# Weight words of block 0 in a PSUM bank, three column tiles converted ahead

## The chip, the cores and the metric

The kernel runs on one core of one Trainium2 chip. The metric is the device time of one execution in microseconds, lower is better. The program is compiled once and run several times; the median counts. A profile is taken in an execution of its own.

## The reference

Three layers follow each other, for 2 sequences of 768 tokens and 512 channels (1536 tokens in all):

```
attention:  8 heads of 64; each token sees the last 128 tokens and the first 4 of its sequence
            scores = q k^T / 8, softmax over the kept ones, times v
dense FFN:  h = x @ w_in        (512 -> 2048)
            g = max(0.01 h, h)
            x = g @ w_out       (2048 -> 512)
router:     8 experts, each token goes to the best one (at most 384 tokens an expert)
            y = gate * relu(x @ w1[e]) @ w2[e]    (512 -> 1024 -> 512)
```

The weights of the dense layer, `w_in` and `w_out`, arrive as 64-bit floats. [...]

## The kernel before

The tokens are cut into 6 blocks of 256 (two tiles of 128). The attention of later tiles and the dense layer of earlier blocks run interleaved: the loop over blocks j holds a loop over 16 column tiles f of the hidden layer, and between them the steps of the attention pipeline are called, so that block 0 of the dense layer works while attention is at tiles 2 and 3. The order on TensorE, ScalarE, GpSimd and SyncE is that of the code; VectorE's order is made by the scheduler of the framework from priorities and dependencies, and then it is a plain queue as well.

In block 0 the dense layer multiplies in full 32-bit form with the converted weights. For column tile f, `first` (L817) forms the product `hps` in a PSUM bank, `leak` (L832) lets ScalarE write 0.01 h (L837) and VectorE the maximum `g` (L838), and two tiles later `second` (L852) adds g times `w_out` to the two banks `y`. From block 1 on the weights are split into two halves `wh` and `wl` (L797, L798).

`convert` (L758) makes the words of column tile f: x = 0 is the piece of `w_in` (raw tile `rawi`), x = 1 that of `w_out` (`rawo`), each 128 x 512 words. Three VectorE operations build a word in place in an SBUF tile `cvt`: `low_word` (L769) shifts and masks the high half, `sign` (L773) ors the sign bit in, `tail` (L777) ors in the top bits of the low half. The six operations of a tile are issued step by step, x = 0 and x = 1 in turn, so that no operation needs the result of the one just before it. They are given a lower priority by `BEHIND` places. `START` names the attention steps at which a conversion begins ahead of block 0; in block 0 one more tile is begun in each of the 16 iterations, so the conversion runs two tiles ahead of the product. The raw tiles have 4 buffers, two column tiles; SyncE loads a pair (0.5 MB each) as soon as the conversion of the pair two tiles before has let go of them.

PSUM has 8 banks: 4 in the pool `ps` for attention, 2 for `y` (`psy`), 2 for `hps` (`psh`). The scores of the first two attention tiles ("plain" ones, `scores_plain`, L635) use `psh` or `psy` before block 0 needs them.

Of the kernel before, what the change touches and what calls it, by code (L numbers as in the profile page):

```python
# [8 lines left out]
F32 = mybir.dt.float32  # L9
F32R = mybir.dt.float32r  # L10
BF16 = mybir.dt.bfloat16
I32 = mybir.dt.int32
AF = mybir.ActivationFunctionType
ALU = mybir.AluOpType
AX = mybir.AxisListType
PSUM = bass.MemoryType.PSUM
DRAM = bass.MemoryType.DRAM

P = 128
# [10 lines left out]
HQ = 3  # L30
SINK = (2, 6)
ROUTER = 3
START = (4, 5)
WARM = 10


RAW = 4
BEHIND = (100, 20)
LAG = 2
SPLIT = (1, 2)  # L40
CLEAR_AT, CLEAR = 8, 2
# [346 lines left out]
class RingAttention(Attention):  # L388
# [246 lines left out]
    def scores_plain(self, t, g):  # L635

        nc = self.nc
        n = t + 1
        mx = self.p["sm"].tile([P, 2, 2], F32, tag="mx", name="mx")
        pss = []  # L640
        for e in range(2):
            d = slice(64 * e, 64 * e + 64)
            if (t * self.NG + g) % 2:
                ps = self.p["psy"].tile([P, 2, n, P], F32, tag=f"y{e}", name="sps")
            else:
                ps = self.p["psh"].tile([P, 2, n, P], F32, tag="h", name="sps")
            for pr in range(2):
                for x in range(n):
                    nc.tensor.matmul(ps[:, pr, x, :], lhsT=self.ident_b, rhs=self.mp[t][:, x * P:(x + 1) * P],
                                     start=True, stop=False)  # L650
                    nc.tensor.matmul(ps[:, pr, x, :], lhsT=self.qk[t, g][d, 2 + pr, :], rhs=self.qk[x, g][d, pr, :],  # L651
                                     start=False, stop=True)
            nc.vector.reduce_max(mx[:, e, :], ps.rearrange("p a n c -> p a (n c)"), axis=AX.X, negate=True)
            nc.vector.tensor_scalar(out=mx[:, e, :], in0=mx[:, e, :], scalar1=self.scale, scalar2=None, op0=ALU.mult)
            pss.append(ps)
        self.pu[t, g] = (pss, mx)
# [58 lines left out]
class FFN:  # L715
# [39 lines left out]
            out=ri, in_=A["moe_w_in"].rearrange("(k p) c -> p k c", p=P)[:, :, f * P * u:(f + 1) * P * u])  # L755
        self.raw[f, x] = ri.rearrange("p k c -> p (k c)")

    def convert(self, f):  # L758

        nc, c = self.nc, self.p["c"]  # L760
        if f >= self.NF:
            return []
        v, w = {}, {}

        def low_word(x):
            r = self.raw[f, x]
            w[x] = r.rearrange("p (n two) -> p n two", two=2)
            v[x] = c.tile([P, 512], I32, tag="c", name="cvt")
            nc.vector.tensor_scalar(v[x], w[x][:, :, 1], 3, 0x3FFFFFF8, op0=ALU.logical_shift_left,  # L769
                                    op1=ALU.bitwise_and)  # L770

        def sign(x):
            nc.vector.scalar_tensor_tensor(v[x], w[x][:, :, 1], -0x40000000, v[x], op0=ALU.bitwise_and,  # L773
                                           op1=ALU.bitwise_or)

        def tail(x):
            nc.vector.scalar_tensor_tensor(v[x], w[x][:, :, 0], 29, v[x], op0=ALU.logical_shift_right,  # L777
                                           op1=ALU.bitwise_or)

        def take(x):  # L780
            r = self.raw.pop((f, x))
            if not self.wide:
                v[x] = c.tile([P, 512], F32, tag="c", name="cvt")
                nc.vector.tensor_copy(v[x], r)
            self.v[f][x] = v[x].bitcast(F32)

        self.v[f] = {}
        calls = [low_word, sign, tail, take] if self.wide else [take]
        return [lambda g=g, x=x: g(x) for g in calls for x in range(2)]

    def split(self, f, x, eng):

# [39 lines left out]
    def leak(self, j, f):  # L832

        nc, N = self.nc, self.N
        ps = self.g[j, f]
        g = self.p["g"].tile([P, N], F32, tag="g", name="g")
        nc.scalar.activation(g, ps, AF.Copy, scale=0.01)  # L837
        nc.vector.tensor_tensor(out=g, in0=ps, in1=g, op=ALU.max)  # L838
        self.g[j, f] = g
# [577 lines left out]
def build(tc, A, n_sink, window, capacity):  # L1417
    nc = tc.nc
# [10 lines left out]
    def pool(st, name, **kw):  # L1429
        p[name] = st.enter_context(tc.tile_pool(name=name, **kw))  # L1430

    with ExitStack() as es:

        work, att, rawst, psy, psh, pst = (ExitStack() for _ in range(6))
        pool(es, "dram", bufs=1, space=DRAM)
        pool(es, "const", bufs=1)
        pool(es, "sm", bufs=3)
# [1 line left out]
        pool(work, "g", bufs=LAG + 1, side="right")  # L1439
        pool(pst, "ps", bufs=4, side="right", space=PSUM)  # L1440
        pool(psy, "psy", bufs=1, side="right", space=PSUM)
        pool(psh, "psh", bufs=2, side="right", space=PSUM)
        es.enter_context(tc.manual_schedule(engines=ORDERED))
        ident = p["const"].tile([P, P], F32, name="ident")
        make_ident(nc, ident)
# [19 lines left out]
        def step(*between):  # L1465

            nonlocal done
            d, pre, mid = steps.pop(0) if steps else (None, (), ())
            for f in (*pre, *between, *mid):
                f()  # L1470
            if d is not None:
                done = d
# [19 lines left out]
        nraw = RAW if ring else 2  # L1492
        pool(rawst, "raw", bufs=nraw, side="right")

        ffn = FFN(nc, p, A, xt, FFN.CAP if ring else FFN.CAP - FEWER // 4)
# [4 lines left out]
        def convert():  # L1500

            nonlocal chunk
            n, chunk = chunk, chunk + 1
            def later(f):
                with tc.high_priority(offset=-BEHIND[started]):
                    f()

            return [lambda f=f: later(f) for f in ffn.convert(n)] + [lambda: [ffn.load(2 * n + nraw + x) for x in range(2)]]

        def some(calls, n):  # L1510
            for f in calls[:n]:
                f()
            del calls[:n]

        conv, started = [], 0
        rt = None
        for n in range(len(steps)):
            if done == TPB - 1:
                break
            if n == ROUTER:  # L1520
                rt = Router(nc, p, A, capacity, ident)
            if n in START:
                conv += convert()
            step(lambda: some(conv, 3))
            some(conv, 3)
        some(conv, 99)
        while chunk < 2:
            some(convert(), 99)
        rt = rt or Router(nc, p, A, capacity, ident)
        started = 1  # L1530
# [16 lines left out]
        def split(n, f=-1, x=0):  # L1547

            while splits and (n > 0 or f >= 0 and x not in ffn.w.get(f, ())):
                ffn.split(*splits.pop(0), nc.vector if j else nc.gpsimd)  # L1550
                n -= 1
# [30 lines left out]
        for j in range(NB):  # L1582
            need = TPB * (j + 2) - 1
            count = next((n + 1 for n, x in enumerate(steps) if x[0] == need), len(steps))
            ndone = 0
            early = j == late and rt.NU
            if j == late:
                att.close()
            if early:
                pool(es, "mx", bufs=1)  # L1590
                ex.start_x()
            for i, f in enumerate(ffn.order(j)):
                if j == 0:
                    conv += convert()
                if j == 1:
                    split(0, f, 0)
                ffn.first(j, f)
                leak = lambda: (some(conv, 2), ffn.leak(j, f), some(conv, 2))
                if ndone < min(count, count * (i + 1) // (ffn.NF - 1)):
                    step(leak)  # L1600
                    ndone += 1
                else:
                    leak()
                more = lambda: ndone < min(count, count * (i + 1) // (ffn.NF - 1))
                some(conv, 2)
                ffn.split_g(j, f, j == late and i >= ffn.NF - ENDG)
                pending.append((j, f, i))
                if len(pending) > LAG:
                    second()
                while more():  # L1610
                    step()
                    ndone += 1
                some(conv, 99)
                split(SPLIT[min(j, 1)])
                if j > 0 or i >= CLEAR_AT:
                    some(clears, max(1, rate) if j else CLEAR)
                if routing and i in ROUTE:
                    routing.pop(0)()
                if early:
                    ex.room = min(ex.RAW + ex.PARTS, 6 + 4 * max(0, i - 1) - (0 if ring else FEWER))  # L1620
                    ex.refill(2)
                    if i == 6:
                        ex.get(0, 0)
                    if i == 11:
                        px = p["ps"].tile([P, DM // P, P], F32, tag="att", name="px")
                        ex.turn(0, 0, px)
                        ex.x_parts(0, 0, px)
            if j == 0:
                rawst.close()
                pool(es, "rt", bufs=2)  # L1630
        def tail():
# [74 lines left out]
```

## Time and profile before

| | |
|---|---|
| median of 3 runs | 650.66 us (650.65 to 652.32) |
| profiled execution | 657.48 us, span 655.8 us |
| TensorE busy in the span | 615.8 us, 94% |
| VectorE busy in the span | 433.5 us, 66% |
| ScalarE, GpSimd busy | 344.9 us, 251.9 us |
| VectorE busy from 60.9 to 143.8 us | 75.09 of 82.9 us |
| TensorE busy from 143.8 to 200 us | 55.59 of 56.2 us |

Busy shares over the whole span mix stages with different limits; a stage is read from a window of its own. Busy times of TensorE have modelled ends, so that 94% is not 94% of its peak. PE is TensorE, DVE is VectorE, ACT is ScalarE, POOL is GpSimd, SP is SyncE. L769 is line 769 of the kernel.

### The profile page before, as it was taken

What the parts mean: (1) busy time and instruction counts of PE and PEld (TensorE: products, weight loads), DVE (VectorE), ACT (ScalarE), POOL (GpSimd) and SP (SyncE); (2) the same over time, 40 slices, a digit from 0 to 9 for tenths busy, and PEclk for the clock granted to TensorE, in tenths of its full rate; (3) what the DMA queues carried; (4) which work ended last, traced back from release to release, by engine and by line L of the source; (5) the groups of instructions that cost most, each with busy time, mean ns of one, the idle gap of its engine ahead of it and who ended that gap; (6) DMA issues with size and microseconds to landing.
All of it is one profiled execution on the core that took longest, in us unless ns stands there. A gap on an engine that the chain in (4) does not pass through costs nothing.

```text
span 655.8 us, 12403 instructions
## 1 busy us (share of the span) xinstructions
PE 615.8 (94%) x4057; PEld 531.2 (81%) x4057; DVE 433.5 (66%) x1031; ACT 344.9 (53%) x997; POOL 251.9 (38%) x451
## 2 busy tenths in 40 slices
PE   9998687989999999999999999999999999996995
PEld 7685555658899999999999998997788888985774
DVE  1499999968986567666766662277366666545871
ACT  4474456558765666655666553255244444434641
POOL 5357596655544545444544443132101001010030
PEclk9598799889999999999999999999899999999898
DMA  9147866942164521141114005756256665446800
GB/s 254 22 147 230 268 190 210 280 134 70 50 241 147 155 56 49 34 145 34 36 39 144 3 10 176 258 177 212 67 182 206 217 201 181 146 132 196 276 14 13
DMA packets 83710, 91.82 MB, mean 140 GB/s; under 512 B 43171, under 2 KB 51363, under 8 KB 83616
## 3 DMA queue, kind: packets, MB, share of 16 engines
q1 hardware_dynamic: 81536, 85.58, 43.1%
q0 software_dynamic: 2080, 5.13, 2.2%
q8 instruction: 41, 0.67, 0.5%
q14 instruction: 53, 0.43, 0.2%
HBM read 71.91 MB, written 20.48 MB: 141 GB/s over the span
## 4 chain that ended last, share of the span: by engine, by line
PE 60%; DVE 17%; issue 9%; ACT 5%; DMA 5%; POOL 2%; SPq 0%; another core or an unknown queue 0%; DVEq 0%; POOLq 0%; ACTq 0%
PE y L867 13%; PE hps L829 13%; PE py L1284 9%; PE ph L1237 8%; PE ops L300 4%; DVE cvt L777 3%; DVE cvt L773 3%; DMA out<-ys,gt 2%; PE sps L651 2%; PE sps L520 2%; DMA craw<-in_moe_w 2%; DVE cvt L769 2%; DVE g L838 2%; PE lps L950 1%; DVE wl L798 1%
## 5 line engine op out<-in xcount | busy, mean ns | idle before, releaser
L867 PE MATMUL y<-wh,gp 128*128 128x512 f32 x320 | 115.1, 400 | 1.0 <-ACT gp L847 1.0
L849 POOL TENSOR_TENSOR gp<-g,gp 128x256 fp32r<-128x256 f32 x77 | 56.8, 738 | 141.9 <-ACT gp L847 129.5
L829 PE MATMUL hps<-xth,wh 128*128 128x256 f32 x320 | 92.7, 290 | 0.0
L1284 PE MATMUL py<-cw,ht 128*128 128x512 f32 x336 | 84.7, 406 | 6.5 <-DVE ht L1274 6.5
L829 PE MATMUL hps<-xtl,wh 128*128 128x256 f32 x320 | 90.2, 282 | 0.0
L829 PE MATMUL hps<-xth,wl 128*128 128x256 f32 x320 | 90.0, 281 | 0.0
L1129 DVE TENSOR_TENSOR cw<-craw,cw 128x512 fp32r<-128x512 f32 x128 | 82.8, 691 | 9.1 <-ACT cw L1127 7.8
L1284 PEld LDWEIGHTS py<-cw,ht 128*128 128x128 f32 x336 | 63.3, 193 | 21.9 <-DVE ht L1274 8.2
L1293 POOL DMA_INDIRECT out<-ys,gt x14 | 17.4, 1244 | 163.8 <-DVE ys L1292 149.5
L1127 ACT CAST cw<-craw 128x512 fp32r<-128x512 f32 x112 | 63.5, 620 | 30.7 <-PE py L1284 30.1
L838 DVE TENSOR_TENSOR g<-hps,g 128x256 f32<-128x256 f32 x96 | 40.2, 418 | 51.5 <-ACT g L837 43.0
L867 PEld LDWEIGHTS y<-wh,gp 128*128 128x128 f32 x320 | 60.0, 188 | 12.3 <-ACT gp L847 1.9
L837 ACT ACTIVATE g<-hps 128x256 f32<-128x256 f32 x96 | 36.4, 379 | 55.1 <-PE hps L829 55.0
L829 PEld LDWEIGHTS hps<-xtl,wh 128*128 128x128 f32 x320 | 60.3, 188 | 3.1 <-issue 0.7
L829 PEld LDWEIGHTS hps<-xth,wh 128*128 128x128 f32 x320 | 60.3, 189 | 3.0 <-issue 0.7
L867 PE MATMUL y<-wl,gp 128*128 128x512 f32 x160 | 62.6, 391 | 0.0
L829 PEld LDWEIGHTS hps<-xth,wl 128*128 128x128 f32 x320 | 60.6, 189 | 0.0
L1237 PE MATMUL ph<-xt,cw 128*128 128x256 f32 (+2 forms) x444 | 58.2, 291 | 1.2 <-DVE xt L1227 0.8
L1237 PEld LDWEIGHTS ph<-xt,cw 128*128 128x128 f32 x444 | 56.6, 189 | 2.0 <-DVE xt L1227 1.5
L213 ACT ACTIVATE pm<-pm,mx 128x132 f32<-128x132 f32 (+1 forms) x80 | 31.7, 398 | 44.3 <-DVE mx L533 44.0
L847 ACT CAST gp<-g 128x256 fp32r<-128x256 f32 x80 | 32.7, 409 | 38.4 <-DVE g L838 31.1
L300 PE MATMUL ops<-pt,vt 128*64 128x128 f32 x456 | 40.8, 233 | 4.9 <-POOL pt L568 4.7
(197 smaller groups left out, 1329.4 us busy)
## 6 DMA issues: line engine op xcount, KB each, us to landing
craw<-in_moe_w SPq DMA_DIRECT2D x128, 256.0 KB
rawi<-in_moe_w_in SPq DMA_DIRECT2D x16, 512.0 KB
rawo<-in_moe_w_out SPq DMA_DIRECT2D x16, 512.0 KB
places<-zero SPq DMA_DIRECT2D x24, 257.0 KB
wh<-wscr SPq DMA_DIRECT2D x16, 256.0 KB
wl<-wscr SPq DMA_DIRECT2D x16, 256.0 KB
xg<-places SPq DMA_DIRECT2D x14, 257.0 KB
natv<-in_v SPq DMA_DIRECT2D x12, 256.0 KB
```

What stands on the lines that cost most here:

```text
L213: nc.scalar.activation(pm[:, e, 0:w], pm[:, e, 0:w], AF.Exp, bias=mx[:, e:e + 1], accum_out=su[:, e:e + 1])
L300: nc.tensor.matmul(ps[:, e, :], lhsT=l, rhs=r, start=(x == 0), stop=(x == len(mm) - 1))
L829: nc.tensor.matmul(ps, lhsT=w, rhs=x, start=(n == 0), stop=(n == len(mm) - 1))
L837: nc.scalar.activation(g, ps, AF.Copy, scale=0.01)
L838: nc.vector.tensor_tensor(out=g, in0=ps, in1=g, op=ALU.max)
L847: nc.scalar.copy(gp[:, 0], g)
L849: eng.tensor_tensor(out=gp[:, 1], in0=g, in1=gp[:, 0].bitcast(F32), op=ALU.subtract)
L867: nc.tensor.matmul(y, lhsT=l, rhs=r, start=(start and n == 0), stop=(stop and n == len(mm) - 1))
L1127: nc.scalar.copy(h, t)
L1129: eng.tensor_tensor(out=l, in0=t, in1=h.bitcast(F32), op=ALU.subtract)
L1237: nc.tensor.matmul(self.ph[f][:, sl], lhsT=w, rhs=self.xt[:, a, k, sl], start=(m == 0), stop=(m == 3 * self.K - 1), skip_group_check=True)
L1284: nc.tensor.matmul(self.py[n], lhsT=x, rhs=w, start=(h == 0 and f == 0 and m == 0), stop=(h == self.NH - 1 and f == self.HF - 1 and m == 2))
```

## The change

In block 0 the word is built in a PSUM bank: `low_word` writes the bank, `sign` works in place there, and `tail` reads it and writes the SBUF tile `cvt`. There is one such bank, and the two words of a column tile are now made one after the other, not in turn. Ahead of block 0 the words are made in SBUF as before, but three column tiles are begun there (START) and not two, so that the conversion runs three tiles ahead. The priority offset in block 0 is 100 instead of 20. The bank is taken from `psh`: in block 0 the product `hps` has one bank, and from block 1 on two again. The plain scores that used the two banks of `psh` in turn take one bank each for their two halves.

```diff
-START = (4, 5)
+START = (3, 4, 5)
...
-BEHIND = (100, 20)
+BEHIND = (100, 100)
...
-                ps = self.p["psh"].tile([P, 2, n, P], F32, tag="h", name="sps")
+                ps = self.p[("psh", "psc")[e]].tile([P, 2, n, P], F32, tag="hu"[e], name="sps")
...
-    def convert(self, f):
+    def convert(self, f, bank):
...
-        v, w = {}, {}
+        v, w, u = {}, {}, {}
 
         def low_word(x):
             r = self.raw[f, x]
             w[x] = r.rearrange("p (n two) -> p n two", two=2)
-            v[x] = c.tile([P, 512], I32, tag="c", name="cvt")
-            nc.vector.tensor_scalar(v[x], w[x][:, :, 1], 3, 0x3FFFFFF8, op0=ALU.logical_shift_left,
+            if bank:
+                u[x] = self.p["psc"].tile([P, 512], I32, tag="u", name="word")
+            else:
+                u[x] = v[x] = c.tile([P, 512], I32, tag="c", name="cvt")
+            nc.vector.tensor_scalar(u[x], w[x][:, :, 1], 3, 0x3FFFFFF8, op0=ALU.logical_shift_left,
                                     op1=ALU.bitwise_and)
 
         def sign(x):
-            nc.vector.scalar_tensor_tensor(v[x], w[x][:, :, 1], -0x40000000, v[x], op0=ALU.bitwise_and,
+            nc.vector.scalar_tensor_tensor(u[x], w[x][:, :, 1], -0x40000000, u[x], op0=ALU.bitwise_and,
                                            op1=ALU.bitwise_or)
 
         def tail(x):
-            nc.vector.scalar_tensor_tensor(v[x], w[x][:, :, 0], 29, v[x], op0=ALU.logical_shift_right,
+            if bank:
+                v[x] = c.tile([P, 512], I32, tag="c", name="cvt")
+            nc.vector.scalar_tensor_tensor(v[x], w[x][:, :, 0], 29, u[x], op0=ALU.logical_shift_right,
                                            op1=ALU.bitwise_or)
...
-        return [lambda g=g, x=x: g(x) for g in calls for x in range(2)]
+        return [lambda g=g, x=x: g(x) for x in range(2) for g in calls]
...
-        pool(psh, "psh", bufs=2, side="right", space=PSUM)
+        pool(psc, "psh", bufs=1, side="right", space=PSUM)
+        pool(psc, "psc", bufs=1, side="right", space=PSUM)
...
-            return [lambda f=f: later(f) for f in ffn.convert(n)] + [lambda: [ffn.load(2 * n + nraw + x) for x in range(2)]]
+            return [lambda f=f: later(f) for f in ffn.convert(n, started)] + [lambda: [ffn.load(2 * n + nraw + x) for x in range(2)]]
...
             if j == 0:
+                psc.close()
+                pool(psh, "psh", bufs=2, side="right", space=PSUM)
                 rawst.close()
```

The lines behind it move: in the changed kernel `low_word`, `sign` and `tail` are L773, L777 and L783, and the maximum is L844. The orders of TensorE, ScalarE and GpSimd stay as they were, and on SyncE one pair of raw loads moves ahead. On VectorE the conversions move. The first place is the start of block 0, from the casts `kT`, which free a bank for attention, to the first maximum `g`. Before:

```order
L163 CAST kT_122<-kps 128x4x4 x2
L777 SCALAR_TENSOR_TENSOR cvt<-rawo,cvt 128x512
L769 TENSOR_SCALAR cvt<-rawi 128x512
L769 TENSOR_SCALAR cvt<-rawo 128x512
L773 SCALAR_TENSOR_TENSOR cvt<-rawi,cvt 128x512
L773 SCALAR_TENSOR_TENSOR cvt<-rawo,cvt 128x512
L838 TENSOR_TENSOR g<-hps,g 128x256
```

The same place on VectorE now, where `word` is the bank:

```order
L163 CAST kT_125<-kps 128x4x4 x2
L777 SCALAR_TENSOR_TENSOR cvt<-rawi,cvt 128x512
L773 TENSOR_SCALAR cvt<-rawo 128x512
L783 SCALAR_TENSOR_TENSOR cvt<-rawi,cvt 128x512
L777 SCALAR_TENSOR_TENSOR cvt<-rawo,cvt 128x512
L777 SCALAR_TENSOR_TENSOR word<-rawi,word 128x512
L783 SCALAR_TENSOR_TENSOR cvt<-rawo,cvt 128x512
L783 SCALAR_TENSOR_TENSOR cvt<-rawi,word 128x512
L773 TENSOR_SCALAR word<-rawo 128x512
L844 TENSOR_TENSOR g<-hps,g 128x256
```

Eight conversion operations stand between the casts and the first maximum instead of five, and by then tile 2 is complete and four of the six operations of tile 3 are done. The second place is the middle of block 0 on VectorE, with buffer numbers. Before, the piece from the sixth maximum:

```order
L838 TENSOR_TENSOR g_901<-hps_881,g_901 128x256
L769 TENSOR_SCALAR cvt_897<-rawi_805 128x512
L769 TENSOR_SCALAR cvt_899<-rawo_807 128x512
L773 SCALAR_TENSOR_TENSOR cvt_897<-rawi_805,cvt_897 128x512
L773 SCALAR_TENSOR_TENSOR cvt_899<-rawo_807,cvt_899 128x512
L532 COPY_PREDICATED pm_921<-sel_174,sps_923 128x128
L532 COPY_PREDICATED pm_921<-sel_174,sps_924 128x128
L777 SCALAR_TENSOR_TENSOR cvt_897<-rawi_805,cvt_897 128x512
L533 TENSOR_REDUCE mx_922<-pm_921 128x2
L777 SCALAR_TENSOR_TENSOR cvt_899<-rawo_807,cvt_899 128x512
```

A piece of the changed kernel's middle, around the seventh maximum:

```order
L777 SCALAR_TENSOR_TENSOR word_1033<-rawi_896,word_1033 128x512
L844 TENSOR_TENSOR g_1036<-hps_1024,g_1036 128x256
L783 SCALAR_TENSOR_TENSOR cvt_1039<-rawi_896,word_1033 128x512
L773 TENSOR_SCALAR word_1069<-rawo_898 128x512
L532 COPY_PREDICATED pm_1056<-sel_177,sps_1058 128x128
L532 COPY_PREDICATED pm_1056<-sel_177,sps_1059 128x128
L777 SCALAR_TENSOR_TENSOR word_1069<-rawo_898,word_1069 128x512
L533 TENSOR_REDUCE mx_1057<-pm_1056 128x2
L783 SCALAR_TENSOR_TENSOR cvt_1074<-rawo_898,word_1069 128x512
L773 TENSOR_SCALAR word_1103<-rawi_1014 128x512
```

One word is taken through its three steps before the next begins, and the next `low_word` stands right behind the `tail` that empties the bank.

## Rows read from the trace of the kernel before

**Rows 1.** Page: busy time of engines, and VectorE's busy tenths in 40 slices.

```profile
PE 615.8 (94%) x4057; PEld 531.2 (81%) x4057; DVE 433.5 (66%) x1031; ACT 344.9 (53%) x997; POOL 251.9 (38%) x451
...
DVE  1499999968986567666766662277366666545871
```

**Rows 2.** Windows: us, busy of PE, PEld, DVE, ACT, POOL; clock, DMA share, GB/s.

```profile
29.40:60.90 31.50, 28.49 (x162) 22.41 (x162) 29.33 (x57) 21.65 (x62) 18.27 (x21) 0.87 0.50 151
...
60.90:143.80 82.90, 66.85 (x358) 47.39 (x357) 75.09 (x145) 43.92 (x138) 59.26 (x74) 0.92 0.75 229
...
143.80:200.00 56.20, 55.59 (x433) 49.59 (x432) 47.85 (x122) 40.51 (x127) 30.37 (x54) 1.00 0.34 113
...
125.00:130.00 5.00, 5.00 (x29) 3.31 (x28) 5.00 (x8) 1.75 (x7) 5.00 (x6) 1.00 1.06 304
```

**Rows 3.** Waits of TensorE from 60.8 to 143.8 us: total, times, longest.

```profile
PE sps L520 <- DVE xtl L311: 8.5, 4, 3.3
PE ops L300 <- POOL pt L568: 4.7, 3, 3.6
```

**Rows 4.** Timeline of VectorE, the fourth, thirteenth and sixteenth maximum: start, duration.

```profile
60.77 0.41 DVE L838 TENSOR_TENSOR g<-hps,g 128x256 f32<-128x256 f32 x1
...
124.50 0.41 DVE L838 TENSOR_TENSOR g<-hps,g 128x256 f32<-128x256 f32 x1
...
143.76 0.42 DVE L838 TENSOR_TENSOR g<-hps,g 128x256 f32<-128x256 f32 x1
```

**Rows 5.** Groups of VectorE by form, 29 to 137 us: busy us, mean ns.

```profile
L777 DVE SCALAR_TENSOR_TENSOR cvt<-rawi,cvt 128x512 int32<-128x512 int32 x16 | 16.6, 1040 | 0.0
L773 DVE SCALAR_TENSOR_TENSOR cvt<-rawo,cvt 128x512 int32<-128x512 int32 x16 | 16.6, 1036 | 0.0
L773 DVE SCALAR_TENSOR_TENSOR cvt<-rawi,cvt 128x512 int32<-128x512 int32 x16 | 15.7, 983 | 0.0
L777 DVE SCALAR_TENSOR_TENSOR cvt<-rawo,cvt 128x512 int32<-128x512 int32 x16 | 14.1, 880 | 0.0
L769 DVE TENSOR_SCALAR cvt<-rawo 128x512 int32<-128x512 int32 x16 | 9.2, 576 | 0.0
L769 DVE TENSOR_SCALAR cvt<-rawi 128x512 int32<-128x512 int32 x16 | 9.2, 572 | 0.1
```

**Rows 6.** Timeline of VectorE and GpSimd at two places of block 0.

```profile
57.44 0.68 DVE L773 SCALAR_TENSOR_TENSOR cvt<-rawo,cvt 128x512 int32<-128x512 int32 x1
57.90 1.37 POOL L798 TENSOR_TENSOR wl<-cvt,wh 128x512 fp32r<-128x512 f32 x1 [3.05 <-ACT wh L797]
58.04 1.77 DVE L777 SCALAR_TENSOR_TENSOR cvt<-rawi,cvt 128x512 int32<-128x512 int32 x1
...
72.49 1.17 POOL L203 TENSOR_TENSOR vt<-natv,vt 128x256 fp32r<-128x256 f32 x1
73.00 0.41 DVE L838 TENSOR_TENSOR g<-hps,g 128x256 f32<-128x256 f32 x1
```

**Rows 7.** Line L571, a PSUM source and an SBUF source: min, median, max ns.

```profile
L571 DVE TENSOR_TENSOR pt<-pps,mown x28: 674/680/681, 147.1 to 399.8; 128x512 fp32r<-128x512 f32 x28
```

**Rows 8.** Groups by form, whole span: a copy out of PSUM.

```profile
L940 DVE COPY x2T<-xps 128x512 f32<-128x512 f32 x12 | 7.8, 683 | 2.3 <-PE xps L938 2.3
```

**Rows 9.** Timeline of VectorE: a row and its dependent one, with the idle time before.

```profile
28.60 0.69 DVE L653 TENSOR_REDUCE mx<-sps 128x2 f32<-128x512 f32 x1 [2.71 <-PE sps L651]
29.32 0.17 DVE L654 TENSOR_SCALAR mx<-mx 128x2 f32<-128x2 f32 x1
```

**Rows 10.** Timeline of TensorE in block 0, products and waits.

```profile
66.47 1.99 PE L829 MATMUL hps<-xth,cvt 128*128 128x256 f32 x8 [1.07 <-DVE cvt L777]
...
130.42 1.89 PE L829 MATMUL hps<-xth,cvt 128*128 128x256 f32 x8
...
135.94 0.51 PE L520 MATMUL sps<-kT,qT 128*128 128x264 f32 x2 [2.93 <-DVE xtl L311]
136.28 3.08 PE L867 MATMUL y<-cvt,g 128*128 128x512 f32 x4
```

More of the change, by code (lines that the diff above doesn't have):

```diff
@@ L1432, in build @@
     with ExitStack() as es:
-        work, att, rawst, psy, psh, pst = (ExitStack() for _ in range(6))
+        work, att, rawst, psy, psh, psc, pst = (ExitStack() for _ in range(7))
         pool(es, "dram", bufs=1, space=DRAM)
```

## The prediction

> **What bounds the kernel now.** I read the page first, then stretches, then the stretch that the change touches. Over the whole span TensorE is busy 94% and VectorE 66% [rows 1], which would make VectorE a side matter. The slices of the same group say otherwise: VectorE stands at 9 in slices 3 to 7 and falls behind later. So the span has stages with different limits, and the change lies in one of them: block 0 of the first dense layer, about 29 to 144 us, where VectorE turns the 64-bit weights into 32-bit words.
>
> The windows [rows 2] give that stage in numbers. From 60.9 to 143.8 us VectorE is busy 75.09 of 82.9 us and TensorE 66.85, at a granted clock of 0.92. From 143.8 to 200 us TensorE is busy 55.59 of 56.2 us at clock 1.00: there TensorE is the limit, it starts block 1 as soon as block 0 ends, and whatever block 0 saves moves everything behind it forward. The waits of TensorE in the stage [rows 3] are 8.5 us for `xtl` (a VectorE row) and 4.7 us for `pt` (GpSimd), so TensorE is fed late.
>
> The pace is read from the row L838, the maximum that ends each column tile's leak, one for each of 16 tiles [rows 4]. The fourth (tile 3) starts at 60.77, the thirteenth (tile 12) at 124.50, the sixteenth at 143.76. The attention steps repeat every three tiles, so 60.77 to 124.50 is three rounds of 21.2 us.
>
> What VectorE does in that time is mostly conversion [rows 5]: 96 operations, 81.4 us in sum, 0.85 us on average. The timeline shows why the average is that high [rows 6]. The L773 row at 57.44 takes 0.68 us. The next, of the same size, takes 1.77 us; it starts while GpSimd runs `wl` (57.90, 1.37 us) and ends after it. Against that the L838 row at 73.00 starts while GpSimd is in `vt` (72.49 to 73.66) and takes its usual 0.41 us; it has an operand in PSUM. The conversions have all their operands in SBUF.
>
> **The change, part by part.** *Price of an operation in the bank.* With one of the two sources or the destination in PSUM I expect what L838 shows, no lengthening by GpSimd. The trace has no VectorE row that writes PSUM. The nearest of this size read it: L571, two sources, 674 to 681 ns in 28 rows [rows 7], and L940, one source, 683 ns [rows 8]. I take 0.68 us for all three operations of a word, since both rows agree. From below the bound is the 0.66 us or so of a short SBUF row (0.68 at 57.44), so nothing to win there; from above it is about 1.2 us, if reading and writing the same bank in place took each column twice (0.53 us more for 512 columns at the 0.27 us that L838's 0.41 and L571's 0.68 differ by for 256).
>
> *From duration to pace.* Rows overlap: the one at 57.44 lasts 0.68 us and the next starts 0.60 us later [rows 6], so 0.08 us of each is covered, and an operation now costs 0.85 - 0.08 = 0.77 us. The bank takes this cover away where an operation needs the result of the one just before it, because one bank holds one word and its three steps follow each other. The maximum at 28.60 (0.69 us) and its dependent row at 29.32 are 0.72 us apart [rows 9], 0.12 us more. In the new order 36 of the 78 operations with a word in the bank stand directly behind another of that chain; before, none did, as two words alternated. So 0.60 + 36/78 x 0.12 = 0.655 us.
>
> *Three rounds, tiles 3 to 12.* By the order there stand 55 conversion operations between the fourth and the thirteenth L838 before and 54 now: 55 x 0.77 - 54 x 0.655 = 7.0 us. The rest of VectorE's rounds is unchanged, so a round shrinks from 21.2 to 18.9 us.
>
> *Up to tile 3.* One more tile is converted ahead: in front of the fourth L838 stand 37 operations instead of 30, some 7 x 0.6 = 4.2 us more. Its cover: two of them move ahead of the row at 28.60, which VectorE reaches after 2.71 us of idling [rows 9], worth 1.0 us; 19 of the 37 are in the bank, 19 x 0.115 = 2.2 us; and the window from 29.4 to 60.9 has 31.5 - 29.3 = 2.2 us of idle [rows 2], which I count as 2.0. That is 5.2 us of cover for 4.2; but the first three maxima stand behind 6, 8 and 10 more operations than before, and each next product must now wait for the maximum. I take a loss of 1 us, between a gain of 1.0 (all the cover holds) and a loss of 4.2 (none does), nearer the first.
>
> *Tail, tiles 12 to 15.* Now 19.3 us with 11 conversions still to do; in the new order 5 are left. VectorE has 6 x 0.77 + 5 x 0.115 = 5.2 us less to do. TensorE's part of it: behind the product of tile 14 at 130.42 it waits 2.93 us for `xtl`, which is queued on VectorE behind conversions, and then runs `y` in 3.08 us at a lower clock [rows 10]. So the gain lies between 2.9 and 5.2 us; I take 4, between them, since TensorE then sets the pace.
>
> *The single bank for `hps`.* In block 0 a product may start only when the maximum of the previous tile is done. Before, the product at 66.47 started ahead of the fifth maximum. This is hidden as long as VectorE is the slower one, and costs nothing then; if TensorE becomes the limit it costs up to the length of leak and maximum per tile (a rival below). The plain scores keep two banks as they had; 0. Loads move one pair earlier on SP; the stage moved 229 GB/s, and 304 GB/s in its fullest stretch [rows 2], so there is room; 0, at most 2 us.
>
> [...]
>
> **The sum.** -1 + 7 + 4 = 10 us. The profiled execution took 657.5 us (span 655.8 and 1.7 around it) and would take 647.5. It is 6.8 us above the median of the runs shown, 650.66; I carry the difference over in microseconds: 640.7 us.
>
> **The rivals.**
> (a) *The rest of the round holds it back.* When VectorE is faster, the attention chain (`pt` from GpSimd, 4.7 us of TensorE's waits) and the tight coupling of product and maximum take part of it: rounds of 20.2 instead of 18.9 us, 3 us in all instead of 7, and 3 of the tail's 4 us: -1 + 3 + 3 = 5 us, 645.7 us. For it: TensorE's busy time is 66.85/82.9 x 21.2 = 17.1 us a round, only 1.8 us under the new VectorE round. Against: its clock was 0.92 there and would rise.
> (b) *Slower through one bank.* Each product waits for the maximum before it, and VectorE is an in-order queue, so a maximum can stand behind two or three conversions (0.66 us each) while TensorE idles. At 1.6 us for each of a round's three tiles, 17.1 + 4.8 = 21.9 us: 0.7 us more a round, 2.1 in three, with the 4.2 us of the start not covered and no gain in the tail +6.3: 657.0 us. It decides from 4.1 us of such waits a round (21.2 - 17.1). Against: TensorE can use most of such a wait for nothing else only if it has run out of attention work and `y`.
> (c) *In place is slow.* If the sign step (bank to the same bank) runs at half rate, 26 x 0.53 = 13.8 us come back: 3.8 us slower, 654.5 us. No row here shows such a form. [...]
> (d) *TensorE alone sets block 0.* Then the stage from 60.9 shrinks at most to its busy time, 16 us: 634.7 us.
>
> **How the numbers follow.** Forecast, gains of 6 to 14 us: 0.55 (637 to 645 us; the 65 ns case is in it with 0.1). (a) 0.20. (d) 0.05. No visible change, gains and losses cancelling: 0.06. (b) 0.08, (c) 0.06. About 0.3% of the time, 2 us, is what a measurement here can tell from no change. Faster 0.55 + 0.20 + 0.05 = 0.80, same 0.06, slower 0.14. The range from 635 to 650 leaves out (b), (c) and little of (d), under 2 in 10.
>
> **What the new profile would show.** Right: L777 and L783 rows with a `word` at 0.66 to 0.70 us with hardly any spread, also while GpSimd runs, and the low-word step at 0.68 instead of 0.41; three rounds of some 19 us between the fourth and the thirteenth maximum; the fourth near 62 us; the sixteenth 8 to 12 us earlier; block 1 as long as before. GpSimd's own rows should be shorter. Wrong: word rows near 1.2 us (c); waits of the `hps` product for the maximum of several us a round (b); TensorE waits for `pt` that grow (a); conversions that wait for their loads; or the gain of block 0 given back after 144 us.

## The result and the profile after

The changed kernel takes 643.8 us in the median of 4 runs (640.25 to 647.39), the kernel before 650.98 in runs beside them (650.65 to 652.32). The ratio is 0.9865 with a 95% interval from 0.9823 to 0.9908: 8.8 us faster, between 6.0 and 11.5. The two medians by themselves differ by 7.2 us, which lies in this interval. The forecast was a gain of 10 us. Each profile below is one execution; the one before took 657.48 us, more than any of the runs just named, so the two traces are compared stage by stage and not as a whole.

The page of the changed kernel, the rows that answer to [rows 1]:

```profile
PE 608.6 (95%) x4057; PEld 526.4 (82%) x4057; DVE 423.6 (66%) x1031; ACT 344.3 (54%) x997; POOL 232.9 (36%) x451
...
DVE  2698999669885666667765662377366665646971
```

VectorE lost 9.9 us of busy time and GpSimd 19.0 us, though GpSimd's order was not touched. The windows, with the columns of [rows 2]:

```profile
29.40:60.90 31.50, 25.77 (x152) 21.19 (x152) 29.13 (x58) 19.30 (x53) 14.13 (x20) 0.87 0.67 200
60.90:143.80 82.90, 74.35 (x436) 53.38 (x436) 68.26 (x154) 52.53 (x167) 49.73 (x87) 0.98 0.79 226
143.80:200.00 56.20, 55.49 (x454) 51.25 (x453) 47.49 (x127) 39.74 (x129) 29.34 (x51) 1.00 0.40 128
```

In the same 82.9 us TensorE now runs 436 matmuls instead of 358, at a granted clock of 0.98 instead of 0.92: block 0 ends earlier, and the start of block 1 has moved into this window. Behind 143.8 us TensorE is full, as before. The timeline of VectorE at the maxima that answer to [rows 4]:

```profile
60.48 0.41 DVE L844 TENSOR_TENSOR g<-hps,g 128x256 f32<-128x256 f32 x1
...
117.38 0.41 DVE L844 TENSOR_TENSOR g<-hps,g 128x256 f32<-128x256 f32 x1
...
132.82 0.42 DVE L844 TENSOR_TENSOR g<-hps,g 128x256 f32<-128x256 f32 x1
```

The windows between these points in the changed kernel:

```profile
60.48:117.38 56.90, 48.35 (x279) 34.30 (x279) 51.89 (x113) 35.10 (x113) 34.83 (x60) 0.99 0.90 260
117.38:132.82 15.44, 15.44 (x84) 10.68 (x83) 9.74 (x27) 9.88 (x32) 8.94 (x17) 0.94 0.63 172
```

Three rounds take 117.38 - 60.48 = 56.9 us (before 63.7) and the tail 15.4 us (19.3). VectorE is busy 51.9 us of the rounds, and in the tail TensorE is full. The sixteenth maximum is 10.9 us earlier. 0.95 us of that is there already at the first product of block 0, which starts at 42.40 us before and at 41.45 now, and this is not the change alone: in the plain scores ahead of it the granted clock fell from 1.00 to 0.50 at another moment of the two executions. From 14 to 16 us, with TensorE busy throughout in both, first before and then in the changed kernel:

```profile
14.00:16.00 2.00, 2.00 (x8) 1.32 (x7) 0.00 (x0) 0.66 (x3) 0.00 (x0) 0.50 1.20 307
14.00:16.00 2.00, 2.00 (x12) 1.26 (x11) 0.61 (x1) 0.60 (x3) 0.00 (x0) 1.00 1.18 305
```

So the start of block 0 is counted from its first product below. From the sixteenth maximum to the end of the span there are 509.8 us, and 512.0 before: what block 0 saved is kept. The other 2.2 us of the 13.2 by which these two spans differ arise near the end, in work that the change does not touch: the last 1389 matmuls took 255.8 us at a granted clock of 0.97 before, the last 1388 took 253.6 us at 0.98 now.

The words themselves, all rows with a tile `word` (minimum, median and maximum in ns), against [rows 5]:

```profile
L773 DVE TENSOR_SCALAR word<-rawi x13: 684/695/702, 39.8 to 116.8; 128x512 int32<-128x512 int32 x13
L777 DVE SCALAR_TENSOR_TENSOR word<-rawi,word x13: 684/695/703, 42.7 to 117.7; 128x512 int32<-128x512 int32 x13
L783 DVE SCALAR_TENSOR_TENSOR cvt<-rawi,word x13: 660/681/698, 43.9 to 118.4; 128x512 int32<-128x512 int32 x13
L773 DVE TENSOR_SCALAR word<-rawo x13: 680/695/720, 44.6 to 119.1; 128x512 int32<-128x512 int32 x13
L777 DVE SCALAR_TENSOR_TENSOR word<-rawo,word x13: 677/693/715, 45.9 to 120.1; 128x512 int32<-128x512 int32 x13
L783 DVE SCALAR_TENSOR_TENSOR cvt<-rawo,word x13: 672/686/703, 46.9 to 121.1; 128x512 int32<-128x512 int32 x13
```

None of the 78 rows is longer than 0.72 us, where a single row of [rows 6] took 1.77. The timeline of the changed kernel at the fourth maximum, with GpSimd's `wl` beside it:

```profile
59.62 1.29 POOL L804 TENSOR_TENSOR wl<-cvt,wh 128x512 fp32r<-128x512 f32 x1 [2.75 <-ACT wh L803]
59.88 0.69 DVE L773 TENSOR_SCALAR word<-rawi 128x512 int32<-128x512 int32 x1
60.48 0.41 DVE L844 TENSOR_TENSOR g<-hps,g 128x256 f32<-128x256 f32 x1
60.81 0.69 DVE L777 SCALAR_TENSOR_TENSOR word<-rawi,word 128x512 int32<-128x512 int32 x1
...
61.53 0.69 DVE L783 SCALAR_TENSOR_TENSOR cvt<-rawi,word 128x512 int32<-128x512 int32 x1
```

Under `wl` the words keep their length. The step at 61.53 needs the one at 60.81 and starts 0.72 us after it; the maximum needs no word and starts 0.60 us after the step at 59.88. So it is throughout block 0: where an operation with a word stands directly behind another of the chain, the two starts are 0.70 to 0.74 us apart (36 pairs); where another operation follows without a wait, 0.59 to 0.62 (40 pairs).

TensorE's waits from 25 to 145 us in the changed kernel, the first row of the view (total, times, longest):

```profile
PE hps L835 <- DVE g L844: 9.1, 5, 2.6
```

The waits of [rows 3] for `xtl` and `pt` are gone, and this one is new: a product that waits for its one bank. 4.4 us of it lie in the start and 4.7 in the three rounds. What it costs, and which part of the change took the others away, is asked below.

### The profile page after: what moved, and what is told of

The parts are those of the page before. It is cut to its first block, busy times and chain, and to the rows that moved or that the text cites. A ratio compares the mean times of both kernels' runs of the same rounds, so it can differ in the third digit from the quotient of the medians.

```text
span 642.6 us, 12431 instructions
## 1 busy us (share of the span) xinstructions
PE 608.6 (95%) x4057; PEld 526.4 (82%) x4057; DVE 423.6 (66%) x1031; ACT 344.3 (54%) x997; POOL 232.9 (36%) x451
## 4 chain that ended last, share of the span: by engine, by line
PE 63%; DVE 16%; issue 10%; DMA 5%; ACT 4%; POOL 1%; another core or an unknown queue 0%; SPq 0%; DVEq 0%; POOLq 0%; ACTq 0%
PE y L873 15%; PE hps L835 15%; PE ph L1243 8%; PE py L1290 8%; PE ops L300 4%; DVE cvt L783 3%; DMA out<-ys,gt 3%; PE sps L520 3%; DVE word L777 2%; PE sps L651 2%; DVE word L773 2%; DVE g L844 1%; PE lps L956 1%; DMA craw<-in_moe_w 1%; PE xps L944 1%
## 5 line engine op out<-in xcount | busy, mean ns | idle before, releaser
L844 DVE TENSOR_TENSOR g<-hps,g 128x256 f32<-128x256 f32 x96 | 40.2, 419 | 51.9 <-ACT g L843 43.4
L835 PEld LDWEIGHTS hps<-xth,wl 128*128 128x128 f32 x320 | 60.6, 189 | 0.0
L835 PE MATMUL hps<-xth,cvt 128*128 128x256 f32 x128 | 32.3, 396 | 9.1 <-DVE g L844 9.1
## 6 DMA issues: line engine op xcount, KB each, us to landing
rawi<-in_moe_w_in SPq DMA_DIRECT2D x16, 512.0 KB
rawo<-in_moe_w_out SPq DMA_DIRECT2D x16, 512.0 KB
```

Of the source, the lines that this page charges most:

```text
L835: nc.tensor.matmul(ps, lhsT=w, rhs=x, start=(n == 0), stop=(n == len(mm) - 1))
```

## The experiments

Each ratio is to runs of the kernel before on the same chip, with its 95% interval. "4th" is the start of the fourth maximum counted from the start of the first product of block 0, "to 16th" the time from the fourth to the sixteenth maximum, both read from the timelines, in us.

| kernel | ratio | interval | 4th | to 16th |
|---|---|---|---|---|
| before | 1 | | 18.4 | 83.0 |
| changed | 0.9865 | 0.9823 to 0.9908 | 19.0 | 72.3 |
| tables alone | 0.9946 | 0.9918 to 0.9974 | 15.0 | 82.3 |
| tables, word by word | 0.9985 | 0.9962 to 1.0008 | 16.7 | 81.5 |
| the same, one `hps` bank | 0.9982 | 0.9956 to 1.0008 | 17.1 | 82.6 |

The last three rows lead step by step from before to the changed kernel; only the bank for the words lies between the last row and the changed kernel. Across the two columns the bank adds 1.9 us at the start and takes 10.2 us off the rest.

### The tables alone

On the kernel before:

```diff
-START = (4, 5)
+START = (3, 4, 5)
-BEHIND = (100, 20)
+BEHIND = (100, 100)
```

> The kernel before with only the two tables changed: three column tiles ahead, and offset 100 in block 0. Words stay in SBUF, hps keeps two banks. Theory (the bank takes the words out of GpSimd's way): word operations stay at 0.85 us on average and single ones above 1.5 us, three rounds stay at 62 to 65 us, the tail behind the thirteenth maximum gains 1 to 3 us and the start loses 0 to 3: ratio 0.995 to 1.005. Rival (the gain is the third tile ahead and the place of the conversions in VectorE's queue): ratio 0.985 to 0.99 as in the changed kernel, three rounds at 57 to 59 us.

3.5 us faster (1.7 to 5.3), just outside the theory's range and well short of the rival's 0.99. The windows of this kernel from the fourth to the thirteenth maximum and to the sixteenth (columns as in [rows 2]):

```profile
55.43:122.65 67.22, 54.10 (x279) 37.85 (x278) 62.44 (x115) 35.10 (x111) 47.55 (x59) 0.87 0.80 240
122.65:137.75 15.10, 14.86 (x84) 10.36 (x83) 11.11 (x27) 10.07 (x34) 12.18 (x18) 1.00 0.72 179
```

The rounds got longer, not shorter (67.2 us against 63.7, where the theory had 62 to 65). The tail got 4.2 us shorter (theory: 1 to 3), and the start 3.3 us, where the theory had no gain. So the two tables together gain at both ends and the rounds give 3.5 us back, while VectorE's word rows stay long (0.83 us on average, the longest 1.77). What the third tile and what the offset of 100 does at the start, no run tells apart.

### Word by word in SBUF, with two banks and with one

The first kernel adds the order of the steps to the one above; the second is the changed kernel with its words in SBUF.

```diff
-        return [lambda g=g, x=x: g(x) for g in calls for x in range(2)]
+        return [lambda g=g, x=x: g(x) for x in range(2) for g in calls]
```

```diff
-ffn.convert(n, started)
+ffn.convert(n, 0)
```

> The kernel before with three column tiles ahead, offset 100, and the two words of a tile made one after the other in SBUF; hps keeps two banks, no word bank. It stands between the run with the tables alone (ratio 0.995, fourth maximum at 55.4 us, rounds 67.2) and the run with the words in SBUF and one hps bank (0.998, 58.3, 66.8). Theory (the single hps bank costs the difference, at the start): fourth maximum within 1 us of 55.4, ratio 0.992 to 0.997. Rival (the order of the words costs it): fourth maximum at 57.5 us or later, ratio 0.996 to 1.001.

> The changed kernel with the words of block 0 built in SBUF; everything else of the change stays: three tiles ahead, one word after the other, one hps bank, the word bank idle. Theory: word operations are back at 0.8 to 0.9 us with a spread to over 1.5, three rounds at 62 to 67 us (55 operations at 0.77 plus 0.12 for each that needs the one before it), the product waits more than the 9.1 us for the maximum; ratio 1.00 to 1.015, so the bank is worth 9 to 18 us. Rival (order and lookahead make the gain): ratio 0.985 to 0.99.

Two rows of the second kernel, groups of VectorE by form from 29 to 140 us (busy us, mean ns):

```profile
L783 DVE SCALAR_TENSOR_TENSOR cvt<-rawi,cvt 128x512 int32<-128x512 int32 x15 | 16.9, 1124 | 0.0
L777 DVE SCALAR_TENSOR_TENSOR cvt<-rawi,cvt 128x512 int32<-128x512 int32 x15 | 13.6, 907 | 0.3
```

In SBUF the words are long again (0.82 us on average over all 96 rows, the longest 1.77), three rounds take 66.8 us, and the ratio is 0.9982, just below the range that the theory gave; the rival's 0.985 to 0.99 is excluded. TensorE's waits in this kernel from 25 to 145 us:

```profile
PE hps L835 <- DVE g L844: 9.4, 6, 3.6
PE sps L520 <- DVE xtl L311: 6.1, 2, 3.4
...
PE ops L300 <- POOL pt L568: 0.4, 1, 0.4
```

The waits for `pt` are nearly gone here too, so it was not the bank that removed them; those for `xtl`, a VectorE row, are still 6.1 us, and only the bank takes them away. The bank for the words is worth 0.9982 - 0.9865, or 7.6 us, with some 3.3 us to either side from the two intervals; the theory had 9 to 18.

Of the two suspects for the loss against the tables alone, the rival of the first run holds: the order of the words costs 0.0039, 2.5 us give or take 2.4, and the fourth maximum comes at 57.8, not 55.4 (1.7 us of this are left when both are counted from the first product). The second `hps` bank is worth nothing that shows while the words are in SBUF: 0.9985 with two, 0.9982 with one, to some 2.3 us.

### GpSimd's subtraction left out

In both kernels `wh` itself stands for `wl` in block 0 (first pair), or a tile of zeros (second pair; the pool `c` has 68 tiles there):

```diff
-        eng.tensor_tensor(out=l, in0=t, in1=h.bitcast(F32), op=ALU.subtract)
+        if eng is nc.gpsimd:
+            l = h
+        else:
+            eng.tensor_tensor(out=l, in0=t, in1=h.bitcast(F32), op=ALU.subtract)
```

> The kernel before without GpSimd's subtraction wl in block 0: wl is the tile wh itself there, so the low halves of these weights are not computed and the values of later blocks differ; the number of TensorE instructions stays. Theory (GpSimd's work lengthens VectorE's operations on SBUF): with 18 us of GpSimd's 75 gone, the mean word operation falls from 0.85 to 0.75 us or less, rows over 1.3 us become rare, and the time falls by 4 to 9 us, ratio 0.986 to 0.994. Rival (the length has another cause, such as the loads that write SBUF): the mean stays at 0.83 to 0.87 us and the ratio within 0.997 to 1.003.

> The changed kernel without the same subtraction (wh in place of wl in block 0, values of later blocks differ). Theory: word operations in the bank stay at 0.68 to 0.70 us, since nothing of GpSimd lengthened them; the ratio to before stays at 0.983 to 0.991, at most 2 us below the changed kernel. Rival (wl is itself what block 0 or 1 waits for): it gains as much here as it gains in the kernel before, 4 us or more below the changed kernel.

The whole times, 1.032 and 1.037 times that of before, answer nothing: with the low halves wrong the values change, the router sends tokens elsewhere, and the expert stage loads 16 groups of tokens instead of 14. Block 0 can be read. From the fourth to the sixteenth maximum the kernel before comes down from 83.0 to 71.1 us, the changed one from 72.3 to 70.6. The mean word operation in SBUF fell from 0.85 to 0.76 us; the rows with a `word` stayed at 0.68 to 0.70. The second pair was made to see this in the whole time:

> The kernel before without GpSimd's subtraction wl in block 0: a tile of zeros stands for wl there (and the pool c has 68 tiles, not 70, to make room for it), so the low halves of these weights are left out, the values shift a little and the routing should stay; the number of TensorE instructions stays. Theory (GpSimd's work on SBUF lengthens VectorE's): as in the run with wh in place of wl, the mean word operation is 0.76 us, three rounds take 56 to 57 us and block 0 ends 11 to 13 us earlier than before; now to be seen in the whole time, ratio 0.980 to 0.988. Rival (the earlier end of block 0 is given back in block 1 or later): ratio 0.993 or more.

> The changed kernel with the same tile of zeros for wl in block 0. Theory: the bank and the missing subtraction remove the same thing, so the second of them adds little: word operations 0.68 to 0.70 us, sixteenth maximum at most 3 us earlier than in the changed kernel, ratio to before 0.981 to 0.987, and equal to the kernel before with zeros within 2 us. Rival (the bank saves something of its own): 4 us or more faster than the kernel before with zeros.

0.9818 (0.9780 to 0.9856) and 0.9831 (0.9793 to 0.9870). Both theories hold in the whole time: without the subtraction the kernel before gains 11.8 us, and the two kernels differ by 0.0013, or 0.8 us, which is less than either interval. From the fourth to the sixteenth maximum they take 69.8 and 69.5 us. Windows of the kernel before with zeros, from the fourth to the thirteenth maximum (shorter than the 56 to 57 us of the theory) and to the sixteenth:

```profile
59.06:114.12 55.06, 48.12 (x279) 35.06 (x278) 52.08 (x114) 34.73 (x112) 33.49 (x50) 0.97 0.93 266
114.12:128.89 14.77, 14.73 (x83) 10.42 (x82) 13.01 (x34) 9.85 (x32) 7.68 (x14) 1.00 1.06 299
```

The three rounds of the kernel before:

```profile
60.77:124.50 63.73, 50.61 (x276) 36.22 (x275) 59.67 (x113) 33.86 (x107) 45.55 (x57) 0.92 0.76 235
```

VectorE does 114 operations in 52.1 us, and did 113 in 59.7 us of the same stretch in the kernel before, with every word in SBUF in both. So the long rows come from GpSimd; the loads, which moved 266 GB/s here and 235 in that stretch before, are not what lengthens them. The timeline of the kernel before says it row by row: of its 64 steps with two sources (L773 and L777), the 16 that GpSimd's rows overlap by 0.04 us at most take 0.67 to 0.69 us, and the 30 that take more than 1.0 us all lie beside GpSimd rows, for 0.93 us or more. In the changed kernel 40 of the 52 such steps in the bank overlap GpSimd rows, and none takes more than 0.72 us. With zeros a part is left: single words still take up to 1.53 us, and GpSimd is still busy with its other work for 33.5 of the 55.1 us of the rounds.

Without the subtraction GpSimd's own queue is shorter too (33.5 us busy in the rounds, not 45.6), which could be a gain of another kind. It is not much of it: TensorE's waits for `pt`, GpSimd's row, only fall from 4.7 to 3.7 us in block 0, while those for `xtl` fall from 8.5 to 1.1.

### The wait for the single bank taken away

The first two products go to the two banks of `y`, free until the third:

```diff
-        ps = self.p["psh"].tile([P, 512], F32, tag="h", name="hps")[:, 0:N]
+        pool, tag = (self.p["psy"], f"y{f}") if j == 0 and f < 2 else (self.p["psh"], "h")
+        ps = pool.tile([P, 512], F32, tag=tag, name="hps")[:, 0:N]
```

> The changed kernel with the first two products hps of block 0 in the two banks of y, which are not used before the third product; so the second and third product need not wait for a maximum. Theory (the single hps bank delays the start: in the changed kernel these two products wait 1.8 and 2.7 us for the maximum before them): second and third product 2 to 5 us earlier, fourth maximum 1 to 2.5 us earlier, ratio 0.981 to 0.985. Rival (VectorE is full there, 5.9 of 6 us from 44 to 50 us, and its queue sets the start): products earlier, fourth maximum unmoved, ratio 0.985 to 0.989 as in the changed kernel.

TensorE in the changed kernel, the second and the third product:

```profile
45.66 1.99 PE L835 MATMUL hps<-xth,cvt 128*128 128x256 f32 x8 [1.77 <-DVE g L844]
50.31 3.06 PE L835 MATMUL hps<-xth,cvt 128*128 128x256 f32 x8 [2.65 <-DVE g L844]
```

and in this one, both without a wait:

```profile
43.30 3.62 PE L836 MATMUL hps<-xth,cvt 128*128 128x256 f32 x16
```

The ratio is 0.9888 (0.9857 to 0.9919), the rival's. The fourth maximum is 2.2 us earlier (1.75 us counted from the first product), which is the theory's, but the rounds take 58.4 instead of 56.9 us, and in them the wait for the bank grows from 4.7 to 5.5 us. So the rounds give 1.5 us of the start back, and of the rest nothing shows in the time, where up to 2 us could hide in the two intervals. The waits of the rounds themselves were not taken away by this run.

### Smaller trials

Two tiles ahead with the bank (START as before):

> The changed kernel with two column tiles ahead (START as before); the bank, the order of the steps, the single hps bank and the offset 100 stay. Theory (the bank is worth some 7 us, the third tile ahead some 3 of its own in SBUF): ratio 0.986 to 0.992, that is 0 to 3 us slower than the changed kernel; fourth maximum 2 to 4 us earlier since six operations fewer stand in front of it, three rounds at 55 to 58 us, the tail 2 to 4 us longer. Rival (the third tile is what lets the bank gain): ratio 0.995 or more, TensorE waiting for words.

0.9889 (0.9845 to 0.9933), as the theory had it. Against 0.9865 the difference is inside the intervals. Its trace is of an execution of 653.7 us, above all its other runs, so its start, rounds and tail are not read from it.

The bank for the words ahead of block 0 too:

```diff
-ffn.convert(n, started)
+ffn.convert(n, 1)
```

> The changed kernel with the bank used for the words ahead of block 0 too, where it is shared with one half of the plain scores. Theory (the words ahead are lengthened by GpSimd too, rows of 0.85 to 1.05 us on average at some steps): these 18 operations come to 0.68 to 0.70 us, the fourth maximum stands 0 to 2 us earlier, ratio 0.982 to 0.988. Rival (the words wait for the scores that hold the bank, or the reverse): fourth maximum 1 to 4 us later, ratio 0.988 to 0.994.

All 96 operations now take 0.68 to 0.70 us on average, and the ratio is 0.9896 (0.9848 to 0.9944): no gain over 0.9865, and in the rival's range. The fourth maximum stands 1.5 us later, but so does the first product, by 1.9 us; counted from there it comes after 18.7 us instead of 19.0, and the table of waits up to the first product has none for the bank. So the rival's wait is not seen either; faster words ahead of block 0 bring its start forward by less than 0.4 us.

Two word banks in turn, one taken from attention, and the old order of the steps:

```diff
-        pool(pst, "ps", bufs=4, side="right", space=PSUM)
+        pool(pst, "ps", bufs=3, side="right", space=PSUM)
-        pool(psc, "psc", bufs=1, side="right", space=PSUM)
+        pool(psc, "psc", bufs=2, side="right", space=PSUM)
```

> The changed kernel with two word banks and the two words of a column tile made in turn again, so that no operation needs the one just before it; the second bank is taken from attention (pool ps has 3 banks, not 4). Theory (a dependent operation directly behind another costs 0.12 us more): the three rounds take 2 to 4 us less than the 56.9 us of the changed kernel, if three attention banks are enough; ratio 0.979 to 0.985. Rival (attention needs its fourth bank, or the pace is set by the loop between product and maximum): rounds of 56 to 60 us, ratio 0.985 to 0.995, with waits for attention banks in it in the first case.

1.0081 (1.0046 to 1.0116): worse than before, and outside both ranges. Waits of TensorE from 62 to 133 us in this kernel:

```profile
PE sps L520 <- ACT pt L566: 5.7, 8, 1.2
PE qps L191 <- ACT kT L160: 2.6, 2, 1.6
```

Both rows of ScalarE empty an attention bank, so attention waits for its banks here. In the later blocks it is TensorE's weight load that waits; from 138 to 460 us, in a row that the tables of the kernel before and of the changed one do not have there:

```profile
PEld sps L520 <- ACT sp L577: 7.2, 25, 0.6
```

The three rounds stay at 56.7 us, although VectorE is busy only 50.2 us of them (51.9 in the changed kernel). What the dependent steps cost in the bank is not settled by this run, since the taken bank covers it.

All splits moved out of block 0 of the kernel before:

```diff
-SPLIT = (1, 2)
+SPLIT = (0, 2)
```

> The kernel before with no splits of weights in block 0 (SPLIT 0 instead of 1): all wh and wl are made in block 1, wl on VectorE there, in time for their products. All values stay. Theory (what the bank saves is GpSimd's contention): block 0 without wl ends 11 to 13 us earlier than before, as with zeros for wl; block 1 has 14 more wl at 0.69 to 0.78 us on a VectorE that was busy 51.7 of 63.2 us, and TensorE fills it: it may lose 0 to 10 us there. Ratio 0.983 to 0.998. Rival (moving wl moves the cost whole): ratio 0.998 to 1.01.

1.0462 (1.0422 to 1.0501), outside both ranges. Block 0 does as the theory says: 70.7 us from the fourth to the sixteenth maximum. Block 1, from the seventeenth maximum to the thirty-third, takes 108.2 us instead of 67.3. Its window in this kernel, and then the first two waits of TensorE over the whole span:

```profile
133.25:241.41 108.16, 84.67 (x532) 71.33 (x531) 68.50 (x158) 56.51 (x166) 38.43 (x62) 0.87 0.29 92
```

```profile
PE hps L829 <- DVE wl L798: 15.2, 15, 1.8
PE hps L829 <- ACT wh L797: 8.3, 9, 2.1
```

The same block in the kernel before:

```profile
146.73:213.98 67.25, 66.64 (x532) 60.30 (x532) 55.55 (x145) 48.06 (x153) 34.32 (x62) 1.00 0.39 126
```

About 23 us of the loss are idle time of TensorE, most of it in these waits, and 18 us are the same 532 matmuls at a granted clock of 0.87 instead of 1.00 (84.67 us busy, not 66.64). That the idling lowered the clock is the author's reading; no run takes the two apart. By count VectorE had some 10 us more to do on 55.6 (13 us more as measured), which 67.3 us would just hold; but by these waits the pieces came late for their products.

None of these kernels is faster than the changed one beyond the intervals.

## Why the prediction was right

**The price of an operation.** Foreseen 0.68 us for all three steps; measured 0.68 to 0.70 in the mean. Rival (c), half rate in place, falls: L777, which reads and writes the bank, takes no longer than L773, which only writes it (0.69 us on average for both). The 65 ns case among the forecast's chances is shown by no run: the steps that read the bank, L777 and L783, take 0.68 to 0.69 us on average, and the same steps with both sources in SBUF 0.67 to 0.69 where GpSimd's rows overlap them by 0.04 us at most (16 rows of the kernel before).

**The cause.** The prediction took GpSimd for it from two pairs of rows. The runs without the subtraction show it, and the overlaps row by row: both kernels come to the same time once GpSimd does less (ratios of 0.9818 and 0.9831). Beside `wl` a step took 0.69 us in the bank and up to 1.77 us in SBUF. `low_word` has one SBUF source and is lengthened too while it writes SBUF: L769 takes 0.41 to 0.43 us with no GpSimd row beside it, and up to 1.50 with one. Writing the bank it takes 0.68 to 0.72 us, with a GpSimd row beside it or not. Why an operand in the bank keeps a row from being lengthened, no run here shows.

**Three rounds.** Foreseen 56.7 us, measured 56.9. The loss of cover for dependent steps (0.055 us on average) is borne out in the spacing of the rows, 0.70 to 0.74 us in 36 pairs against 0.60; its price in time was not measured. The sum comes out by two differences that cancel: VectorE is busy 7.8 us less in the rounds (59.7 to 51.9) and not 7.0, and idle 0.9 us more. In SBUF the order of the words costs 2.5 us in the time; in the traces 1.7 us of it stand at the start and none in the rounds. Rival (a), with rounds of 20.2 us or 60.6 in all, falls.

**The start.** Foreseen a loss of 1 us; counted from the first product it is 19.0 - 18.4 = 0.7 us. Its make-up was not foreseen, and that the number fits is luck: the prediction had the third tile ahead as a cost and the words in the bank as cover for it. Measured, the two tables by themselves gain 3.3 us, the order takes 1.7 back, the one bank 0.4, and the words in the bank cost 1.9. The last fits the low-word step at 0.69 instead of 0.41 us, two operations more ahead of the fourth maximum (37, not 35), and waits for the single bank of 1.8 and 2.7 us instead of 1.4 and 1.6; how much each of the three makes is not shown.

**The tail.** Foreseen 4, measured 3.8 us. It belongs to the lookahead, as counted: the tables alone bring 4.2 us there, with the words still in SBUF.

**The single bank.** Costed at nothing if VectorE stays the slower one. TensorE waits 9.1 us for it, so rival (b) has its mechanism; its price does not show. With the words in SBUF, where TensorE waits 9.4 us for it, a second bank brings nothing; in the changed kernel two borrowed banks take away the 4.4 us of waits at the start and the time does not fall. The 4.7 us in the rounds were never taken away with the words in the bank, so for them it is argued and not shown: VectorE is busy 51.9 of the 56.9 us there and TensorE 48.4, and VectorE's own waits in the rounds are for ScalarE's `pm` (3.0 us) and `qT` (0.5), none for the maximum.

**The sum.** -0.7 + 6.8 + 3.8 = 9.9 us by the maxima of these two executions, against 10 foreseen; the ratio says 8.8, and the median of 643.8 us lies 3.1 above the 640.7 foreseen. The gain is not given back: block 1 takes 67.3 us before and after. Rival (d) would have TensorE full in block 0; in the rounds it is busy 48.4 of 56.9 us.

Two things in the prediction are not right as they stand. VectorE's nines are in slices 3 to 8, and one more in slice 11. And its range of 635 to 650 us leaves out more than it says: (b) and (c) are 0.14, and the points of (d), 634.7 us, and of no visible change, 650.7, lie outside as well, which makes up to 0.25.

## What to carry to other kernels

When one form of VectorE row shows a wide spread (0.66 to 1.77 us for one size), look at what GpSimd does in the same microseconds before counting the mean as its price; here an operand in PSUM took the spread away (0.66 to 0.72 us in 78 rows), and less GpSimd work brought the mean word operation from 0.85 to 0.76 us. A long wait in the table of waits is worth what a run without it gains: here 4.4 of the 9.1 us were taken away, and the time did not fall. Work moved to a stage where TensorE is full must be finished ahead of its use; here a block with waits of up to 2.1 us for `wl` and `wh` lost some 23 us as idle time and 18 us at a granted clock of 0.87 instead of 1.00.

## What the hardware showed beside that

GpSimd's rows were longer beside the words in SBUF, too. Its groups by form from 29 to 137 us in the kernel before:

```profile
L568 POOL TENSOR_SCALAR_AFFINE_SELECT pt<-pt 128x512 fp32r<-128x512 f32 x15 | 13.8, 943 | 0.0
...
L542 POOL CAST psk<-ph 128x8 fp32r<-128x8 f32 x8 | 4.5, 561 | 0.0
```

and in the changed kernel:

```profile
L568 POOL TENSOR_SCALAR_AFFINE_SELECT pt<-pt 128x512 fp32r<-128x512 f32 x16 | 9.8, 636 | 2.5 <-ACT pt L566 2.5
...
L542 POOL CAST psk<-ph 128x8 fp32r<-128x8 f32 x9 | 1.9, 215 | 0.0
```

GpSimd's `affine_select` took 943 ns on average beside VectorE's words in SBUF and 636 ns beside the words in the bank, without any change to GpSimd's code. One cast of 128 x 8 elements (L542) went from 561 to 215 ns, but two others of the same size that follow it (L543, L544) only from 238 to 215 and from 273 to 192, so the small size alone does not decide the loss. The 4.7 us of TensorE's waits for `pt` [rows 3] are not explained by this: with the words in SBUF and the rest of the change they are 0.4 us, while the `affine_select` still takes 910 ns.
